# One written order for the whole first phase of an attention and expert kernel, with one v tile for the tail tokens of two batches

## The chip, the core and the metric

The kernel runs on one NeuronCore of one Trainium2 chip. The metric is device time in microseconds (us). The engines are PE (TensorE; its weight loads are PEld), DVE (VectorE), ACT (ScalarE), POOL (GpSimd) and SP, whose queue issues nearly all DMAs. Each engine takes its instructions in the order in which they stand in its queue.

## What is computed

Three layers follow each other, for 4 batches of 576 tokens:

```python
# 1. attention, 8 heads of 64, causal window of 128, ALiBi bias
scores = q @ k.T / 8 + slope * -(t - s)      # masked outside 0 <= t-s < 128
x = softmax(scores) @ v                      # [4, 576, 512]
# 2. gated layer
h = relu(x @ w_in); u, v = h[..., :512], h[..., 512:]
v_n = (v - mean(v)) / sqrt(var(v) + 1e-6)    # per token
v_s = w_spatial @ v_n + b_spatial            # mixes the 576 tokens
y = (u * v_s) @ w_out
# 3. four experts of full causal attention, gated by the top 2 logits
out = sum_e gate_e * (softmax(causal(q_e k_e.T / 8)) @ v_e) @ wo_e
```

All products run in a split of two parts (high and low) and three passes (high by high, high by low, low by high; `PASSES`, line 37), except the attention of layer 1 and the transposes.

## The kernel before

576 tokens are four tiles of 128 and a tail of 64 (`TOK`, line 34). A tile of layer 1 is (batch b, tile j), 20 of them. **The first phase** does layer 1 and the part of layer 2 up to the product u * v_s, which goes to DRAM (`g_dram`). **The fold** (`fold`, line 800 and after) multiplies w_out into the expert weights. **The second phase** does layer 3.

In the first phase each tile passes through these steps, with the names that the written order gives them: scores on PE (`s`, psum `ps`, two buffers), row minimum on DVE and exponential on ACT (`l`, `e`), division (`f`, three DVE instructions), transposes on PE (`t`, psum `pt`) and their copy on ACT (`c`), masking by POOL (`g`), the product with v (`a`, psum `px`), and the split of the result into x high (`xh`, ACT, line 498) and x low (`xl`, DVE, line 164). `pt` and `px` share a pool of one buffer (`psT`): transposes cannot start while an earlier `px` is still being read by `xh` and `xl`. Then layer 2: `V`, 12 products of 512 columns for each tile of 128 tokens (line 524), `r`, `bn`, `ag`, `n`, `N` (relu, mean and variance, normalising and splitting on ACT and DVE), `U` (288 columns, 12 products for each of four feature blocks and two halves of the tokens, line 588) and `P` (the mixing over tokens, 14 products each, lines 615 and 618), with `pm` multiplying by u. Opening work beside this: `C0` to `C7` decode the eight chunks of w_in from 64-bit numbers and split them (two ACT copies, five DVE steps and three products each), `W` splits w_spatial, and four chunks of w_out are decoded in the same way.

Two things set the order. `OPENING` is a text of single steps in the order of issue; all engines follow it, up to about tile 6. After it a loop over the remaining tiles (lines 730 and after) issues attention steps at fixed places, and between them pulls V, U and P products from a list (`Dense`, whose `pull` hands out work by estimated cost). There only PE follows the program's order; the queues of ACT, DVE, POOL and SP are ordered by a scheduler that simulates the program when it is built. `out_weights` (four chunks of w_out) is one of the things that the loop steps through. `idle` and `warm` add transposes of the identity, whose results are not used.

A tail tile has 64 tokens, but its V products are as long as those of a whole tile: the 64 tokens stand twice among the 128 columns of the loaded operand (`take`, the 640-column `x`), since the second copy is needed by the mixing in split form.

Of the kernel before, what the change touches and what calls it, by code (L numbers as in the profile page):

```python
# [37 lines left out]
OPENING = """
    k0 q0 q1 raw0 raw1 raw2 raw3 k1 k3 k4 k5 s0.0 s0.1 C0.abs v0 l0.0.0 l0.1.0 e0.0.0 C0.max e0.1.0 l0.0.1 C0.shl v1 C1.abs l0.0.2 C0.or e0.0.2 e0.0.1
    C1.max C0.sum+17 v2 C0.mask l0.0.3 C0.mul e0.0.3 l0.1.1 C2.abs C0.add raw4 f0.0.add l0.1.2 f0.0.rec l0.1.3 C0.high f0.0.mul s1.1+2 v3 e0.1.2 C1.shl  # L40
    e0.1.3 k2 C2.max C0.minus e0.1.1 t0.0 v4 l1.1.cp C0.low s1.0 f0.1.add C1.or c0.0 f0.1.rec l1.1.0 C1.sum f0.1.mul e1.1.0 l1.0.cp t0.1 l1.1.1 q2 c0.1
    l1.1.2 l1.1.3 l1.0.0 e1.1.1 q3 l1.0.1 a0 e1.0.0 l1.0.2 l1.0.3 e1.0.1 q4 C1.mask C2.shl e1.0.3 reltail C1.mul xh0 e1.0.2 C2.or C1.add e1.1.2 f1.0.add
    xl0 C2.sum C3.abs raw5 e1.1.3 f1.0.rec C2.mask C1.high f1.0.mul C3.max C1.minus t1.0 f1.1.add C2.mul C1.low c1.0 f1.1.rec C3.shl raw6 s2.1+2 C4.abs
    f1.1.mul C3.or s2.0 C4.max C3.mask t1.1 q5 C4.shl C3.sum l2.0.cp g1.0.0 c1.1 C4.or C2.add C2.high l2.1.cp g1.1.0 C4.sum g1.0.1 l2.0.0 l2.0.1 e2.0.0
    C2.minus l2.0.2 g1.1.1 l2.0.3 e2.0.1 l2.1.0 l2.1.1 C2.low C4.mask a1+4 e2.1.1 C3.mul e2.1.0 C4.mul raw7 C5.abs l2.1.2 W0.ld e2.0.2 l2.1.3 C5.max
    C3.add e2.1.2 W1.ld s4.0 e2.1.3 C5.shl v5 C3.high C5.or s4.1 C6.abs f2.1.add l4.0.cp C3.minus xh1 f2.1.rec C5.sum C5.mask f2.1.mul C3.low C4.add
    e2.0.3 C6.max V0.0 C4.high C5.mul f2.0.add C6.shl V0.1 C7.abs f2.0.rec xl1 W0.hi C5.add C7.max W1.hi C4.minus f2.0.mul t2.1 C5.high V0.2 W1.lo c2.1
    C7.shl C4.low C5.minus W0.lo t2.0 r0 V1.0 C7.or C5.low W2.ld c2.0 bn0 g2.1.0 W3.ld C7.sum g2.0.0 l4.0.0 ag0 l4.0.1 e4.0.0 V1.1 l4.1.cp g2.1.1 e4.0.1
    l4.1.0 l4.1.1 g2.0.1 e4.1.0 f4.0.add s3.1 f4.0.rec e4.1.1 C7.mask C6.or a2 C7.mul W2.hi C6.mask W3.hi l3.1.cp V1.2 W3.lo xh2 v6 C6.mul C7.add r1
    C6.sum l3.1.0 l3.1.1 C7.high l3.1.2 l3.1.3 s5.1 e3.1.1 f4.0.mul e3.1.3 C7.minus f4.1.add xl2 C6.add e3.1.0 s3.0 f4.1.rec e3.1.2 W2.lo C7.low t4.0  # L50
    f3.1.add f4.1.mul W4.ld C6.high V2.0 f3.1.rec l3.0.cp W5.ld c4.0 f3.1.mul q6 t4.1 C6.minus c4.1 V2.1 q7 l3.0.0 g4.0.0 C6.low l3.0.1 g4.1.0 l3.0.2
    e3.0.0 l3.0.3 g4.0.1 t3.1 l5.1.0 e3.0.1 l5.1.1 g4.1.1 U0.2.0 l5.1.2 e3.0.2 l5.1.3 bn1 e3.0.3 U0.2.1 c3.1 U0.0.0 f3.0.add ag1 f3.0.rec e5.1.0 f3.0.mul
    U0.2.2 e5.1.3 g3.1.0 s6.1 e5.1.2 e5.1.1 g3.1.1 W5.hi t3.0 f5.1.add l6.1.cp U0.0.1 f5.1.rec l6.1.0 U0.0.2 c3.0 f5.1.mul e6.1.0 s6.0 W5.lo ur0.0 ur0.2
    l6.1.1 g3.0.0 W4.hi V2.2 l6.1.2 l6.1.3 e6.1.2 l6.0.cp g3.0.1 a4 e6.1.3 W4.lo e6.1.1 r2 f6.1.add l6.0.0 s5.0 f6.1.rec xh4 l6.0.1 bn2 U0.1.0 e6.0.1 q8
    xl4 U0.1.1 e6.0.0 U0.1.2 f6.1.mul t5.1 ag2 l6.0.2 ur0.1 l6.0.3 U0.3.0 n2.ln l5.0.0 c5.1 l5.0.1 U0.3.1 l5.0.2 e6.0.3 l5.0.3 U0.3.2 e6.0.2 e5.0.1 a3
    f6.0.add e5.0.3 f6.0.rec f6.0.mul e5.0.2 ur0.3 n2.ex e5.0.0 n2.r0 V4.0 n2.r1 xh3 v7 f5.0.add n2.r2 f5.0.rec n2.r3 f5.0.mul v8 V4.1 xl3 N0.sc V4.2
    N1.sc N0.hi N2.sc t5.0 N1.hi N0.lo V3.0 c5.0
"""
# [1159 lines left out]
```

## Time and profile before

| | |
|---|---|
| median of 3 runs (lowest, highest) | 497.64 us (497.02, 500.23) |
| profiled execution, its own time | 497.51 us |
| its span, first to last instruction | 495.8 us |
| PE busy (share of the span) | 480.6 us (97%) |
| DVE, ACT, POOL busy | 305.5, 262.7, 101.2 us |
| mean granted TensorE clock | 0.993 |

The span is what the trace shows; the execution's own time is 1.7 us longer. "Busy" of PE counts a matmul until its modelled end, and matmuls overlap, so the distance from the start of one matmul to the start of the next tells what it costs. A number in brackets after "idle before" or behind an arrow says how long an engine stood idle and which instruction ended that.

### The profile page before, as it was taken

How to read it: one execution, taken by the hardware profiler on the slowest of the kernel's cores; microseconds unless marked ns; L12 is line 12 of the kernel's file. 1: busy time of each engine (PE TensorE's matmuls, PEld its weight loads, DVE VectorE, ACT ScalarE, POOL GpSimd, SP SyncE). 2: the span in 40 equal slices, each digit the busy share in tenths (PEclk: the TensorE clock that was granted, in tenths of full speed). 3: DMA queues.
4: the chain of work that ended last, by engine and by line, in shares of the span. 5: the costliest groups of instructions: out<-in, count | busy, mean ns of one | idle time of the engine just before them, and what ended most of it. 6: DMA issues, size and time to landing. Idle time of an engine off the chain costs nothing.

```text
span 495.8 us, 10569 instructions
## 1 busy us (share of the span) xinstructions
PE 480.6 (97%) x3919; PEld 422.5 (85%) x3919; DVE 305.5 (62%) x1082; ACT 262.7 (53%) x782; POOL 101.2 (20%) x210
## 2 busy tenths in 40 slices
PE   7889999999999998999999999999999999999997
PEld 6467789997889987899888999998899899897875
DVE  3899888645977657775455524365484564556352
ACT  3777976523655445653345314256575545545554
POOL 3032402211202221021211010112322243223110
PEclk9899999999999998999999999999999999999999
DMA  7963233145204431300305550330000000001223
GB/s 240 342 189 118 82 97 117 47 134 173 66 32 141 149 138 42 98 25 27 111 1 189 190 189 2 97 96 1 2 23 2 2 22 1 1 1 66 85 86 107
DMA packets 24631, 43.77 MB, mean 88 GB/s; under 512 B 5634, under 2 KB 8066, under 8 KB 24196
## 3 DMA queue, kind: packets, MB, share of 16 engines
q1 hardware_dynamic: 24436, 42.97, 26.4%
q8 instruction: 31, 0.51, 0.4%
q14 instruction: 20, 0.16, 0.1%
q10 hardware_dynamic: 144, 0.13, 0.1%
HBM read 31.55 MB, written 11.53 MB: 87 GB/s over the span
## 4 chain that ended last, share of the span: by engine, by line
PE 84%; DVE 7%; DMA 3%; ACT 3%; SPq 2%; issue 1%; ACTq 0%
PE pg L615 10%; PE pq L910 10%; PE pv L524 10%; PE pu L588 7%; PE pvB L934 6%; PE pxB L1042 5%; PE pout L1077 5%; PE ptB L1021 5%; PE px L486 5%; PE psB L975 4%; PE ps L411 4%; PE pw L809 3%; PE pt L455 3%; PE pg L618 2%; DMA q<-in_qP 2%; DMA k<-in_kP 2%
## 5 line engine op out<-in xcount | busy, mean ns | idle before, releaser
L187 ACT ACTIVATE p<-p,st 128x128 f32<-128x128 f32 x144 | 56.3, 393 | 26.5 <-DVE st L186 26.3
L524 PE MATMUL pv<-win,x 128*128 128x512 f32 x240 | 63.1, 404 | 0.7 <-ACT x L498 0.7
L910 PE MATMUL pq<-x,W 128*128 128x288 f32 x384 | 58.3, 302 | 0.8 <-DVE k L164 0.8
L615 PE MATMUL pg<-wsp,vn 128*128 128x288 f32 x384 | 58.9, 298 | 0.0
L588 PE MATMUL pu<-x,win 128*128 128x288 f32 x384 | 57.1, 304 | 0.0
L910 PEld LDWEIGHTS pq<-x,W 128*128 128x128 f32 x384 | 52.0, 189 | 3.6 <-DVE k L164 1.5
L464 POOL TENSOR_SCALAR_AFFINE_SELECT pU<-pT 128x512 f32<-128x512 f32 (+1 forms) x32 | 23.2, 726 | 154.5 <-ACT pT L457 144.2
L588 PEld LDWEIGHTS pu<-x,win 128*128 128x128 f32 x384 | 53.6, 193 | 1.2 <-ACT vn L557 0.3
L615 PEld LDWEIGHTS pg<-wsp,vn 128*128 128x128 f32 x384 | 52.9, 188 | 1.3 <-issue 1.3
L524 PEld LDWEIGHTS pv<-win,x 128*128 128x128 f32 x240 | 43.1, 188 | 11.4 <-issue 1.8
L199 POOL TENSOR_SCALAR pB<-pB,stB 128x384 f32<-128x384 f32 (+4 forms) x64 | 36.0, 582 | 70.3 <-DVE stB L998 53.8
L187 ACT ACTIVATE pB<-pB,stB 128x128 f32<-128x128 f32 (+3 forms) x64 | 35.6, 558 | 20.3 <-DVE stB L186 20.3
L934 PE MATMUL pvB<-W,x 128*128 128x260 f32 (+1 forms) x240 | 34.3, 289 | 0.0
L186 DVE CUSTOM_DVE_ANT_0 pB<-psB,trit 128x128 f32<-128x128 f32 (+3 forms) x64 | 28.2, 485 | 9.6 <-PE psB L975 9.2
L186 DVE CUSTOM_DVE_ANT_0 p<-ps,relm 128x128 f32<-128x128 f32 x128 | 29.9, 284 | 5.2 <-PE ps L411 4.6
L934 PEld LDWEIGHTS pvB<-W,x 128*128 128x128 f32 (+1 forms) x240 | 29.9, 178 | 1.7 <-issue 1.7
L411 PE MATMUL ps<-k,q 64*128 64x256 f32 (+1 forms) x256 | 30.6, 374 | 0.5 <-DMA q<-in_qP 0.5
L1021 PE MATMUL ptB<-ident,pB 128*128 128x128 f32 (+1 forms) x200 | 31.0, 275 | 0.0
L457 ACT COPY pT<-pt 128x512 f32<-128x512 f32 (+1 forms) x40 | 21.6, 540 | 15.5 <-PE pt L455 14.5
L1077 PE MATMUL pout<-wo,o 128*128 128x512 f32 x102 | 29.3, 412 | 0.0
L536 DVE BATCH_NORM_STATS2 vs<-vr 128x6 f32<-128x512 f32 x20 | 13.8, 692 | 24.0 <-ACT vr L533 24.0
L1042 PE MATMUL pxB<-pTB,vt 128*64 128x128 f32 (+2 forms) x480 | 28.3, 262 | 0.0
(162 smaller groups left out, 894.4 us busy)
## 6 DMA issues: line engine op xcount, KB each, us to landing
q<-in_qP SPq DMA_DIRECT2D x20, 256.0 KB, 2.9
g_dram<-g SPq DMA_DIRECT2D x16, 288.0 KB, 2.1
...
```

Of the source, the lines that this page charges most:

```text
L186: lambda: nc.vector.tensor_tensor_reduce(s_view, ps_view, tab, -0.125, FLT_MAX, ALU.add, ALU.min, nm),
L187: lambda: nc.scalar.activation(s_view, s_view, AF.Exp, bias=nm, scale=-1.0, accum_out=sm),
L199: nc.gpsimd.tensor_scalar(p, p, r, 0.0, op0=ALU.mult, op1=ALU.add)
L411: nc.tensor.matmul(ps[:, o, 256 * h : 256 * h + kn], Q_[b, j][r, hp, :], K_[b][r, hp, k0 : k0 + kn], start=True, stop=True)
L524: nc.tensor.matmul(pv, x[i][:, k, t0 : t0 + P], win[j][:, k, 512:1024], start=(n == 0 and k == 0), stop=(n == 2 and k == 3))
L588: nc.tensor.matmul(pu[:, :HALF], win[i][:, k, m * P : (m + 1) * P], x[j][:, k, c], start=(n == 0 and k == 0), stop=(n == 2 and k == 3))
L615: nc.tensor.matmul(pg[:, :HALF], vn[i][k][:, m * P : (m + 1) * P], wsp[j][:, k, c], start=(n == 0 and k == 0), stop=False)
L910: nc.tensor.matmul(pq[:, :HALF], W[i][:, k, c0 : c0 + P], G[j][:, k, c], start=(n == 0), stop=(n == 11))
L934: nc.tensor.matmul(pv[:tn, :260], G[i][:, k, COL[t] : COL[t] + tn], W[j][:, k, 512:772], start=(n == 0), stop=(n == 11))
L1021: nc.tensor.transpose(pt[:kb, n, :], p[pr][:, o, c0 : c0 + kb], ident)
L1042: nc.tensor.matmul(px[64 * o : 64 * o + 64, pr, :qn], vt[:kb, c, (2 * pr + o) * 64 : (2 * pr + o) * 64 + 64], rhs, start=(c == 0), stop=(c ...
L1077: nc.tensor.matmul(po[:tn], o2[i][:, pr, :tn], wos[j][:, pr, :], start=(n == 0), stop=(n == 5))
```

## The change

**The written order covers the whole first phase.** `OPENING` now has 1286 steps instead of 414 and ends at the last tile; `FIRST` and `SECOND` hold the rest (the last V, U and P products). The loop over tiles, `v_tile`, `u_half`, `spatial`, `normalised`, `out_weights` and `now`/`xready` are gone. Up to the end of `OPENING` every queue (ACT, DVE, POOL, SP) follows the text. Step names carry the batch now (`V0.4.2` is batch 0, tile 4, pass 2), `gs` is the store of u * v_s, and `O` are the steps of w_out's chunks. At the start the SP queue loads the first chunk of w_in ahead of the first two q tiles, and k of batch 1 behind w_in's seventh chunk instead of its fourth.

**Tail tokens of two batches share one V tile.** Odd batches run their tail first (`ORDER`). x has 704 columns: the tail stands at columns 0 to 63 (so that U reads 576 columns in a row) and again at 576 to 639 for an even batch, 640 to 703 for an odd one. V of tile 4 of batch 0 covers both tails, likewise batch 2; there is none for batches 1 and 3. The normalised rows go to four tiles `vt2` by ACT and DVE copies of halves. w_spatial and b_spatial are rolled by 64 on the way in, and u * v_s is read back by one DMA instead of two.

```diff
+ORDER = ((0, 1, 2, 3, 4), (4, 0, 1, 2, 3))
 OPENING = """
...
+    k0 raw0 q0 q1 raw1 raw2 raw3 k2 v0 T1 T0 C0.abs v1 C0.max C0.shl s0.1+10 v2 C0.or s0.0 l0.1.0 l0.1.1 C0.sum e0.1.0 l0.1.2 l0.0.0 e0.1.1 k1 l0.0.1
...
```

```diff
-    x = [xg.tile([P, 4, 640], F32R, name=f"x{i}") for i in range(2)]
+    x = [xg.tile([P, 4, 704], F32R, name=f"x{i}") for i in range(2)]
     u = [d2.tile([P, S], F32, name=f"u{m}") for m in range(4)]
-    vn = [[d2.tile([P, 512], F32R, name=f"vn{i}_{t}") for t in range(5)] for i in range(2)]
-    back, over = u[0][:, :P], u[1][:, :P]
+    vn = [[d2.tile([P, 512], F32R, name=f"vn{i}_{t}") for t in range(4)] for i in range(2)]
+    vt2 = [[d2.tile([P, 512], F32R, name=f"vt{r}_{i}") for i in range(2)] for r in range(2)]
+    back, over, first = (u[i][:, :P] for i in range(3))
+    nc.gpsimd.affine_select(out=first, in_=back, pattern=[[-1, P]], fill=FAR, **below)
+    for h in range(H):
+        nc.vector.tensor_scalar(relm[:, 0, h, :], first, -8.0 * 2.0 ** -(h + 1.0), None, op0=ALU.mult)
...
                 nc.sync.dma_start(K_[b][:, :, q0 : q0 + qn], kP[b, :, :, q0 : q0 + qn])
-            elif j == 0:
+            elif j == ORDER[b % 2][0]:
         if "v" in parts:
-            V_[b, j] = a1.tile([P, 512], F32, tag="v", name=f"v{b}_{j}", bufs=5)
-            if j == 4:
-                nc.gpsimd.memset(V_[b, j][qn:], 0.0)
-            nc.sync.dma_start(V_[b, j][:qn], v[b, q0 : q0 + qn])
+            for t in ((j,) if b % 2 == 0 or j < 3 else (3, 4) if j == 4 else ()):
+                t0, tn = TOK[t]
+                kept = b % 2 and t > 2
+                V_[b, t] = vtail[b % 2] if t == 4 else a1.tile([P, 512], F32, tag="w" if kept else "v", name=f"v{b}_{t}", bufs=1 if kept else 5)
+                nc.sync.dma_start(V_[b, t][:tn], v[b, t0 : t0 + tn])
...
     def take(b, j, px, parts=(0, 1)):
         q0, qn = TOK[j]
         if j < 4:
-            to = [t[:, :, q0 : q0 + P] for t in x]
+            to = [t[:, :, 64 + q0 : 64 + q0 + P] for t in x]
         else:
-            to = [t[:, :, 512:640].rearrange("p m (r c) -> p m r c", r=2) for t in x]
+            to = [t.rearrange("p m (r c) -> p m r c", c=64)[:, :, 0 : 10 + b % 2 : 9 + b % 2, :] for t in x]
             px = px[:, :, :64].unsqueeze(2).to_broadcast([P, 4, 2, 64])
         if 0 in parts:
             nc.scalar.copy(to[0], px)
         if 1 in parts:
             lo_part(to[1], px, to[0])
-            xready[b, j] = now[0]
...
-        t0 = TOK[t][0]
+        t0 = 64 + TOK[t][0]
...
         def high(t):
-            nc.scalar.copy(vn[0][t], vr[t])
+            if t < 4:
+                nc.scalar.copy(vn[0][t], vr[b, t])
+                return
+            both, odd = vt2[0][1], slice(64, 128)
+            nc.scalar.copy(both, vr[b, t])
+            nc.scalar.copy(vt2[0][0][0:64], vr[b, t][0:64])
+            for i in range(2):
+                nc.scalar.copy(vt2[1][i][0:64], vr[b, t][odd])
 
+            if t < 4:
+                lo_part(vn[1][t], vr[b, t], vn[0][t])
+                return
+            both, odd = vt2[0][1], slice(64, 128)
+            lo_part(vt2[1][1][odd], vr[b, t][odd], both[odd])
+            lo_part(both[odd], vr[b, t][0:64], both[0:64])
...
-                    nc.tensor.matmul(pg[:, :HALF], vn[i][4][:kn, m * P : (m + 1) * P], wsp[1 - i][:kn, 4, c], start=False, stop=(i == 1))
+                    nc.tensor.matmul(pg[:, :HALF], vt2[b % 2][i][:kn, m * P : (m + 1) * P], wsp[1 - i][:kn, 4, c], start=False, stop=(i == 1))
...
-    tiles = [(b, j) for b in range(B) for j in range(5)]
-    ops_ = {}
+    tiles = [(b, j) for b in range(B) for j in ORDER[b % 2]]
...
     with tc.manual_schedule(engines={E_.Activation, E_.DVE, E_.Pool, E_.SP}):
-        warm(28)
+        warm(15)
         for name in OPENING.split():
             step(name)
-    decoded[0] = 9
-    for name, names in (("u0_0", FIRST), ("u0_1", SECOND), ("s0", THIRD)):
+    for name, names in (("u3_1", FIRST), ("s3", SECOND)):
         dense.add(rest(names), cost(names), name=name)
-    for b in range(1, B):
...
-    def parts(s):
-
-        if s >= 9:
-            next(outw, None)
-
-    RATE = 8200.0
-    outw = iter(())
-    for s in range(7, len(tiles) + 2):
-        now[0] = 4 * s
-
-        tc.no_sync_barrier()
-        if s == 9:
-            early_stack.close()
-            outw = out_weights(right.enter_context(tc.tile_pool(name="later", bufs=1, side="right")))
-        if s > 2:
-            b, j = tiles[s - 2]
-            if j in (0, 2) and b > 0:
-                dense.through(f"u{b - 1}_{j // 2}")
-            px = attend(b, j)
-        if s < len(tiles):
-            scores(*tiles[s])
-        if s > 2:
-            take(*tiles[s - 2], px)
-        if 4 <= s + 2 < len(tiles):
-            load_chunk(*tiles[s + 2])
...
-        nc.sync.dma_start(f[:, :, 64:576], src[:, :, 0:512])
-        nc.sync.dma_start(f[:, :, 0:64], src[:, :, 512:576])
+        nc.sync.dma_start(f, src)
```

(The new `out_ops` issues the same instructions for a chunk of w_out as `out_weights` did, one step each.)

PE, the last V tiles of the program (`pv`; x high and low are x_106 and x_107, w_in's two parts win_102 and win_103). Before, batch 3 ends with its tail tile:

```order
L524 MATMUL pv_4_3181<-win_102,x_106 128x512 x4
L524 MATMUL pv_4_3181<-win_103,x_106 128x512 x4
L524 MATMUL pv_4_3181<-win_102,x_107 128x512 x4
L588 MATMUL pu_0_1_3200<-x_106,win_102 128x288 x4
L588 MATMUL pu_0_1_3200<-x_107,win_102 128x288 x4
L588 MATMUL pu_0_1_3200<-x_106,win_103 128x288 x4
```

Now the last V tile is tile 3 of batch 3, between two passes of a P product (`pg`):

```order
L555 MATMUL pv_3_3114<-win_102,x_106 128x512 x4
L555 MATMUL pv_3_3114<-win_103,x_106 128x512 x4
L555 MATMUL pv_3_3114<-win_102,x_107 128x512 x4
L633 MATMUL pg_3_0_3056<-wsp_104,vn_0_116 128x288
L633 MATMUL pg_3_0_3056<-wsp_104,vn_1_117 128x288
L633 MATMUL pg_3_0_3056<-wsp_104,vn_2_118 128x288
L633 MATMUL pg_3_0_3056<-wsp_104,vn_3_119 128x288
L636 MATMUL pg_3_0_3056<-wsp_105,vt_0_120 128x288
L636 MATMUL pg_3_0_3056<-wsp_104,vt_1_121 128x288
L618 MATMUL pu_0_1_3144<-x_106,win_102 128x288 x4
L618 MATMUL pu_0_1_3144<-x_107,win_102 128x288 x4
L618 MATMUL pu_0_1_3144<-x_106,win_103 128x288 x4
```

In all, PE has 240 products in V before and 216 now.

PE, from the product with v of tile (2, 3) on (`px_3`). Before, the next user of the same psum buffer is the transpose `pt_4`:

```order
L486 MATMUL px_3_2296<-pT_3_1_2241,v_3_1689 64x128 x2
L411 MATMUL ps_0_0_2313<-k_2017,q_0_2015 128x128 x4
L411 MATMUL ps_0_1_2318<-k_2017,q_0_2015 128x128 x4
L588 MATMUL pu_0_0_2290<-x_107,win_102 128x288 x4
L588 MATMUL pu_0_0_2290<-x_106,win_103 128x288 x4
L588 MATMUL pu_1_0_2344<-x_106,win_102 128x288 x4
L455 MATMUL pt_4_0_2349<-ident,p_4_0_2214 128x128 x2
L588 MATMUL pu_1_0_2344<-x_107,win_102 128x288 x4
```

Now:

```order
L529 MATMUL px_3_2311<-pT_3_1_2146,v_3_1505 64x128 x2
L555 MATMUL pv_2_2286<-win_102,x_107 128x512 x4
L462 MATMUL ps_0_1_2339<-k_1414,q_0_1873 128x128 x4
L462 MATMUL ps_1_1_2347<-k_1414,q_1_2046 128x256 x4
L529 MATMUL px_4_2355<-pU_4_0_2259,v_3_1505 64x64 x2
L529 MATMUL px_4_2355<-pT_4_0_2258,vtail_162 64x64 x2
```

The scores of the next tiles and a pass of V stand between `px_3` and the next user of the buffer, which is now another `px`, that of the tail tile.

DVE, where w_out's first chunk is decoded (`wo`, `fo`, `rawo`). Before, the first of these steps stand behind the products with u of batch 0 (`g`):

```order
L621 TENSOR_TENSOR g_1_1223<-u_109,pg_1_0_1224 128x288
L438 TENSOR_TENSOR p_3_1_1287<-p_3_1_1287,st_3_1_1288 128x512
L621 TENSOR_TENSOR g_1_1223<-u_109,pg_1_1_1255 128x288
L621 TENSOR_TENSOR g_2_1281<-u_110,pg_2_0_1282 128x288
L621 TENSOR_TENSOR g_2_1281<-u_110,pg_2_1_1313 128x288
L329 TENSOR_SCALAR fo_1432<-fo_1432 128x512
L330 TENSOR_SCALAR wo_1431<-fo_1432 128x512
L164 TENSOR_TENSOR x_107<-px_2_1340,x_106 128x4x128
```

Now the chunk's steps stand ahead of the division of the tail tile of batch 1 (`p_4_0`, `p_4_1`), among the normalising of batch 0 (`vs`, `vr`):

```order
L579 SCALAR_TENSOR_TENSOR vs_458<-vs_458 128x3
L384 SCALAR_TENSOR_TENSOR wo_719<-rawo_658,wo_719 128x512
L580 TENSOR_TENSOR vs_458<-vs_458 128x3
L385 TENSOR_SCALAR fo_720<-wo_719 128x512
L581 TENSOR_SCALAR vs_458<-vs_458 128x3
L487 TENSOR_TENSOR st_0_0_786<-st_0_0_786,tiny 128x4
L386 SCALAR_TENSOR_TENSOR fo_720<-rawo_658,fo_720 128x512
L582 TENSOR_TENSOR vs_458<-vs_458 128x3
L213 TENSOR_TENSOR x_107<-px_3_792,x_106 128x4x128
L586 TENSOR_SCALAR vr_1_586<-vr_1_586,vs_458 128x512
```

The chunk moved from among batch 0's P products to a place ahead of all of them.

## Rows read from the trace of the kernel before

**Rows 1.** The page: span, and busy time of each engine.

```profile
span 495.8 us, 10569 instructions
...
PE 480.6 (97%) x3919; PEld 422.5 (85%) x3919; DVE 305.5 (62%) x1082; ACT 262.7 (53%) x782; POOL 101.2 (20%) x210
```

**Rows 2.** Timeline of PE, opening: start, length, engine, line, operation, tiles, count.

```profile
39.75 0.39 PE L279 MATMUL psw<-win,minus 128*128 128x512 f32 x1
39.98 0.60 PE L455 MATMUL pt<-ident,p 128*128 128x128 f32 x4
40.33 1.17 PE L524 MATMUL pv<-win,x 128*128 128x512 f32 x4
...
45.09 1.13 PE L411 MATMUL ps<-k,q 64*128 64x256 f32 x8
46.15 0.44 PE L486 MATMUL px<-pU,v 128*64 128x128 f32 x4
...
48.05 1.19 PE L524 MATMUL pv<-win,x 128*128 128x512 f32 x4
...
70.20 3.02 PE L524 MATMUL pv<-win,x 128*128 128x512 f32 x12
73.05 0.60 PE L455 MATMUL pt<-ident,p 128*128 128x128 f32 x4
```

**Rows 3.** Groups of instructions: shape, count, busy us, mean ns, idle us before.

```profile
L524 PE MATMUL pv<-win,x 128*128 128x512 f32 x240 | 63.1, 404 | 0.7 <-ACT x L498 0.7
```

**Rows 4.** Waits of PE: total us, times, longest us.

```profile
PE pt L455 <- DVE x L164: 4.0, 4, 2.1
...
PE pv L524 <- ACT x L498: 0.7, 1, 0.7
```

**Rows 5.** Chain of waits, 180 to 200 us: start, length, what.

```profile
186.68 1.45 DVE vr L554 x3
188.13 0.60 DVE wo L331
188.73 0.60 DVE vn L164
...
189.76 0.61 DVE x L164
...
190.50 0.41 PE pt L455 x2
```

**Rows 6.** Two stretches: busy us by engine, TensorE clock, DMA share.

```profile
core 0: us, PE busy (x) PEld busy (x) DVE busy (x) ACT busy (x) POOL busy (x), PEclk, DMA share, GB/s
12.40:62.00 49.60, 46.40 (x294) 32.07 (x295) 45.49 (x170) 38.94 (x122) 12.38 (x16) 0.97 0.58 183
186.00:198.40 12.40, 10.32 (x68) 9.71 (x66) 9.84 (x35) 7.37 (x26) 2.10 (x4) 0.86 0.14 42
```

**Rows 7.** Timeline of DVE, opening.

```profile
30.54 0.69 DVE L429 COPY_PREDICATED ps<-lowt,ps 128x512 f32<-128x512 uint16 x1
31.13 0.28 DVE L186 CUSTOM_DVE_ANT_0 p<-ps,relm 128x128 f32<-128x128 f32 x1
31.34 0.28 DVE L186 CUSTOM_DVE_ANT_0 p<-ps,relm 128x128 f32<-128x128 f32 x1
...
38.13 0.15 DVE L436 TENSOR_TENSOR st<-st,tiny 128x4 f32<-128x4 f32 x1
38.20 0.42 DVE L330 TENSOR_SCALAR u<-f 128x512 int32<-128x512 int32 x1
38.54 0.16 DVE L437 RECIPROCAL st<-st 128x4 f32<-128x4 f32 x1
```

**Rows 8.** Timeline of ACT and DVE: the first chunk of w_in.

```profile
9.88 0.69 ACT L328 ACTIVATE f<-raw 128x512 f32<-128x512 f32 x1 [7.28 <-DMA raw<-in_w_in]
...
10.60 0.43 DVE L329 TENSOR_SCALAR f<-f 128x512 f32<-128x512 f32 x1 [1.57 <-ACT f L328]
```

**Rows 9.** Timeline of PE: the first product of the weight fold.

```profile
287.98 12.23 PE L809 MATMUL pw<-wc,wt 128*128 128x386 f32 x68
```

More of the change, by code (lines that the diff above doesn't have):

```diff
@@ L42 @@
[L42 to L53, printed above, removed]
@@ L237, in block_kernel @@
         nc.gpsimd.memset(pad[r : r + 1, :], 1.0)
+    for r in range(2):
+        nc.gpsimd.tensor_scalar(vt2[r][0][64:97], pad[64:97].to_broadcast([33, 512]), 1.0, 0.0, op0=ALU.mult, op1=ALU.add)
     early_stack = ExitStack()
-    decoded = [0]
     early = early_stack.enter_context(tc.tile_pool(name="early", bufs=4, side="right"))
@@ new lines, in out_ops, with get, start, high @@
+    def out_ops(k, pool):
+        c = slice(k * P, (k + 1) * P)
+        wide = w_outT.dtype == I64
+        wide = w_outT.dtype == I64
+        raw = pool.tile([P, 512], w_outT.dtype, tag="raw", name=f"rawo{k}", bufs=2)
+        ops, tiles = {}, {"w": raw}
+        def get(n, dtype, tag="f", bufs=3):
+            tiles[n] = pool.tile([P, 512], dtype, tag=tag, name=f"{n}o{k}", bufs=bufs)
+            return tiles[n]
+        def start():
+            if wide:
+                w, f = get("w", F32, "w", 2), get("f", F32)
+                ops.update(word_ops(w, f, raw, f))
+                ops["abs"]()
+        def high():
+            nc.scalar.copy(get("hi", F32R), tiles["w"])
+        def low():
+            lo_part(get("lo", F32R), tiles["w"], tiles["hi"])
+        for n in ("max", "shl", "or", "mask", "mul"):
+            ops[n] = lambda: None
+        ops["ld"] = lambda: nc.sync.dma_start(raw, w_outT[c, :])
+        ops["add"] = lambda: nc.vector.tensor_add(tiles["w"], tiles["w"], tiles["f"]) if wide else None
+        ops["sh"] = lambda: nc.sync.dma_start(wt_dram[0, k], tiles["hi"].bitcast(F32))
+        ops["sl"] = lambda: nc.sync.dma_start(wt_dram[1, k], tiles["lo"].bitcast(F32))
+        ops["abs"], ops["hi"], ops["lo"] = start, high, low
+        return ops
@@ L374, in block_kernel @@
     Q_, K_, V_ = {}, {}, {}
+    vtail = [a1.tile([P, 512], F32, name=f"vtail{i}", bufs=1) for i in range(2)]
+    for t in vtail:
+        nc.gpsimd.memset(t[64:], 0.0)
     def load_chunk(b, j, parts="qkv"):
@@ L439, in softmax_ops @@
         return ops
-    def softmax(b, j, g):
-        for op in softmax_ops(b, j, g).values():
-            op()
     def transpose_ops(b, j, g):
@@ L467, in transpose_ops @@
         return ops
-    def transposes(b, j, g):
-        for op in transpose_ops(b, j, g).values():
-            op()
     def attend(b, j):
@@ L569, in normal_ops @@
         return ops
-    def normalised(st, tiles):
-        ops = normal_ops(st, tiles)
-        yield lambda: (ops["ln"](), ops["ex"]())
-        yield lambda: [ops[f"r{i}"]() for i in range(4)]
-        for t in tiles:
-            for name in ("sc", "hi", "lo"):
-                yield ops[f"{name}{t}"]
     def u_ops(b, s, m):
```

256 lines of the change are left out of this document (117 added, 139 removed).

## The prediction

> **What bounds the kernel now.** I read the busy times first: PE is busy for 480.6 of 495.8 us, DVE for 305.5 [rows 1]. The reader is to see that all other engines have room on average, so a change pays what it takes off PE's queue, and costs what it makes PE wait. Second, the timeline of PE in the opening gives prices that the busy times don't: the distance from one start to the next, since matmuls overlap [rows 2]. Third, the waits of PE: transposes wait four times, 4.0 us in all and 2.1 at the longest, for DVE's x low, and V once, 0.7 us, for ACT's x high [rows 4]. Fourth, the chain of waits around the longest of them shows why: x low at 189.76 stands in DVE's queue behind the scaling of three V tiles, a step of w_out's decoding and a split of V; the transposes that want its buffer start at 190.50 [rows 5]. Fifth, the table of stretches: from 186.0 to 198.4 the granted clock averages 0.86, so after this wait PE was at 1.2 GHz for a share of 0.28 of it and did (1 - 0.86) x 12.4 = 1.7 us less work than at 2.4 [rows 6]. In the opening it is different: from 12.4 to 62.0 us DVE is busy for 45.49 of 49.6 us, 4.1 idle, and PE's early work hangs on it [rows 6].
>
> All sums are made against the profiled execution's own 497.51 us, 1.7 above its span and 0.1 below the median of 497.64.
>
> **Part 1: 24 products of V less.** The instruction lists have 240 and 216. Twelve such products take 73.05 - 70.20 = 2.85 us, 0.2375 each [rows 2]; busy time over count gives 63.1 / 240 = 0.263 [rows 3]. So 24 are worth 5.7 to 6.3 us; I take 5.7, since the distance between starts is what PE's queue pays. V lies on PE's queue in stretches that DVE and ACT don't hold up, so all of it counts. The relu, statistics and scaling that go with two dropped V tiles, and the extra half copies into vt2, are on ACT and DVE after the opening and hide behind PE, which is busy there without a break.
>
> The Trainium skill ("TensorE: Matmul & The Clock Gate", section "Back-to-back issue gap") gives some 131 ns for a 512-column product in a sustained stream. By that the part would be worth 24 x 0.131 = 3.1 us and the sum 490.2; this trace does not agree, with 237 ns.
>
> **Part 2: the waits of PE behind the loop.** At the place of the longest wait the old order leaves two score groups and three U passes between `px_3` and the transposes; the new one leaves a pass of V (0.95) and two score groups, one of them whole at 46.15 - 45.09 = 1.06 [rows 2], at least 2.4 us. What must fit in is x high and x low; x low takes 0.61 [rows 5], and x high I put at the same length, so 1.3 us with the handing over. The order in which ACT and DVE take them matters more than the room: old x low stood behind five other DVE instructions, because only PE was held to the program there. In the written text, for tiles 9 to 19, I added up PE's work between each `a` and the next use of the buffer: never under 1.9 us (after a9 and a12), and x low has at most a few instructions ahead of it. So the waits should go. Bounds: nothing goes (0), or all goes: 4.0 + 0.7 [rows 4] + 1.7 of clock [rows 6] = 6.4. I take 5.0, near the upper end, and leave 1.4 for new short waits, since twenty hand-overs on fixed queues will not all be met. With PE no longer stopped for 2.1 us the clock should hold; if some other stop of that length appears, the 1.7 comes back.
>
> **Part 3: the opening.** Here PE follows DVE, so I compare how far DVE's queue is ahead of PE's at the points where PE needs it. Distances on DVE: a 512-column step 31.13 - 30.54 = 0.59, the fast kind 38.54 - 38.20 = 0.34, a row minimum 0.21, a small one 0.07, say 0.08 [rows 7]. On PE: a score group 1.06, the product with v 48.05 - 46.15 = 1.9, a conversion pass 0.23, a turn 0.35, a V pass 0.95 [rows 2]. Before, the largest lead is at the transposes of the tail tile (t4.1): ahead of them DVE has 39 long, 24 fast, 32 minima and 18 small ones, 23.0 + 8.2 + 6.7 + 1.4 = 39.3 us; PE has 11 score groups (five of them short, 0.5), 25 filling transposes (0.09), 31 conversion passes (0.24), seven turns, three products with v (tile 0's is 1.0) and seven V passes, 32.3 us. Lead 7.0. Now it is at the tail tile of batch 1 (t5.1), which V of the shared tile needs: DVE has 59 long, 27 fast, 44 minima and 33 small ones, 55.8 us, w_out's first chunk among them; PE has 15 score groups (eight short), 27 fillers, 32 conversion passes, eleven turns, five products with v, twelve V passes and six U passes (0.53, by columns), 47.2 us. Lead 8.6, so PE waits 1.6 us longer. Against it: the first chunk of w_in lands at 9.88 now and DVE stood idle 1.57 us for it [rows 8]; two q loads no longer stand ahead of it on SP's queue, which gives back between nothing and 1.6. I take the middle, +0.8. Bounds: DVE's 4.1 idle us [rows 6] and the 1.6 with them may shrink or double, -4 to +6. The shorter warm-up (28 to 15) and other fillers stand where PE waits for the first data; I cost them at nothing, covered by that wait.
>
> **Costed at nothing.** K of batch 1 behind more of w_in, and the stores `gs` on SP's queue, ahead of loads of tiles that are wanted at least a tile later. The pads on POOL (101.2 us busy) [rows 1]. The rolled weights (on the way in) and one DMA instead of two for reading back, which end under the last P products.
>
> **Sum.** 497.5 - 5.7 - 5.0 + 0.8 = 487.6 us.
>
> **The rivals.**
> (a) The waits come back elsewhere: part 2 gives 0, with part 3 at +0.8 to +2.4. Time 492.6 to 494.2. For it: ACT and DVE queues that are fixed can hold PE at other tiles; against it: the room counted above. Chance 0.20.
> (b) The opening gets shorter too: DVE's sum up to the last decoding step of the half of w_in that V reads falls from 20.9 (18 long, 15 fast, 22 minima, 8 small) to 15.5 us (13, 12, 16, 4), so V can begin some 5 us earlier. If a good half of that survives the later lead, part 3 is -3; with part 2 at its full 6.4: 497.5 - 5.7 - 6.4 - 3.0 = 482.4. For it: the idle 4.1 us of DVE; against it: the lead of 8.6, which no earlier V removes. Chance 0.14.
> (c) Slower: one late step on a fixed queue holds all behind it. The place is the hand-over px, x high, x low, next use of the buffer, in all 20 tiles; the price is what the four recorded waits cost on average, 1.0 us [rows 4]. If all 20 paid it, 20 - 4 = 16 us more and the clock loss stays: 497.5 - 5.7 + 0.8 + 16 = 508.6. It decides from the fifth waiting tile more than now: 497.5 - 5.7 + 0.8 leaves 4.9 us to lose. For it: a tile waits now with 2.6 us of PE work between (two short score groups and three U passes); against it: DVE is free for 38% of the span [rows 1]. Chance 0.10.
> (d) The dropped products are worth half their distance, because those that stay then stand as far apart as their neighbours' weight loads demand: 24 x 0.119 = 2.9 us, 490.4 in sum. Against it: the twelve in the row stand 237 ns apart. Chance 0.04.
> (e) That the change doesn't do what it says: the instruction lists show 24 products fewer and the new order on every queue, so only an unnoticed reordering of the parts after the opening text remains; it has no price of its own and no chance here.
> The forecast, 484.5 to 491.5, has 0.52.
>
> **The numbers.** 487.6 us; range 482.5 to 495.0, which takes in the forecast, (a), (d) and about half of (b), some 0.83. About 1%, 5 us, is what a measurement of this kernel can tell: faster below 492.7, from the forecast, (b), (d) and a part of (a): 0.73; within 1%, most of (a) and the mild end of (c): 0.19; slower 0.08.
>
> **What would show it.** Part 1: 216 products in V's group and still 230 to 240 ns from start to start. Part 2: the wait of transposes for x low gone from PE's list, and no second stretch at 1.2 GHz after the opening. Part 3: the first product of the shared V tile is reached with PE's total wait in the opening within 2 us of the old one. Together: the fold's first product, at 287.98 before [rows 9], starts near 278; what follows it is unchanged in code, so nearly the whole difference must stand there. The prediction is wrong if PE shows new waits of over 3 us in sum behind the opening, if the fold starts later than 283, or if the second phase changes by more than 1 us.

## The result and the profile after

| | before | after |
|---|---|---|
| median (lowest, highest) | 497.85 us (497.02, 500.23), 4 runs | 483.7 us (483.63, 485.17), 4 runs |
| profiled execution, its own time | 497.51 us | 483.76 us |
| its span | 495.8 us | 482.0 us |
| PE busy | 480.6 us | 471.5 us |

The ratio is 0.9715, 95% interval 0.9677 to 0.9753. The change takes 13.8 us off the profiled execution, against 9.9 forecast: 483.7 is in the range and 3.9 below the 487.6.

The page of the changed kernel, for [rows 1]: PE's share is 98% now, DVE's work is nearly the same, and in the 40 slices of the granted clock none is below 9.

```profile
span 482.0 us, 10496 instructions
...
PE 471.5 (98%) x3884; PEld 413.5 (86%) x3884; DVE 304.2 (63%) x1084; ACT 262.3 (54%) x780; POOL 95.0 (20%) x206
...
PEclk9999999999999999999999999999999999999999
```

The fold's first product, for [rows 9] (duration minimum, median, maximum, then the first and the last start):

```profile
L773 PE MATMUL pw<-wc,wt x96: 333/339/344, 274.2 to 291.0; 128*128 128x386 f32 x96
```

It starts at 274.2 in place of 287.98, so all of the 13.8 us stand ahead of it. What follows is as long as before: 482.0 - 274.2 = 207.8 us against 495.8 - 287.98 = 207.8.

The longest waits of PE, for [rows 4]:

```profile
PE psw L328 <- DVE st L487: 1.7, 1, 1.7
PE warm L347 <- POOL ident masks.py:199: 1.6, 1, 1.6
PE ps L462 <- DMA q<-in_qP: 0.9, 1, 0.9
PE pq L873 <- DVE k L213: 0.8, 1, 0.8
PE pt L502 <- ACT pT L504: 0.5, 1, 0.5
```

Neither the transposes' wait for x low nor V's for x high is there. Of these rows only `pq` lies behind 62 us, in the second phase: from 62.0 to the fold the list of PE's waits is empty, and the table of stretches shows PE busy for the whole of it (columns as in [rows 6]; the first row answers to the opening there, the second to the place of the old longest wait):

```profile
12.40:62.00 49.60, 47.38 (x353) 33.65 (x353) 47.33 (x172) 39.23 (x122) 10.39 (x16) 1.00 0.74 256
186.00:198.40 12.40, 12.40 (x119) 11.17 (x118) 8.38 (x39) 7.91 (x32) 1.67 (x4) 1.00 0.01 2
...
62.00:274.20 212.20, 212.20 (x1731) 191.86 (x1730) 141.08 (x483) 110.88 (x348) 32.77 (x58) 1.00 0.27 92
```

The group of V, for [rows 3], and a run of 12 of its products on PE's timeline, for [rows 2]:

```profile
L555 PE MATMUL pv<-win,x 128*128 128x512 f32 x216 | 56.1, 400 | 0.0
```

```profile
37.08 3.02 PE L555 MATMUL pv<-win,x 128*128 128x512 f32 x12
39.94 0.60 PE L502 MATMUL pt<-ident,p 128*128 128x128 f32 x4
```

24 products fewer, and (39.94 - 37.08) / 12 = 0.238 us each, as before.

DVE's first work, for [rows 7, 8]. Before, a first part of it stands in [rows 8]: the first step of w_in's chunk at 10.60 us, after 1.57 us without work. Ahead of that there was a longer gap, which the prediction has no row for:

```profile
2.64 1.21 DVE L227 TENSOR_SCALAR relm<-u 128x128 bf16<-128x128 f32 x8
8.40 0.29 DVE L186 CUSTOM_DVE_ANT_0 p<-ps,relm 128x128 f32<-128x128 f32 x1 [4.55 <-PE ps L411]
```

After:

```profile
4.60 2.00 DVE L280 TENSOR_SCALAR relm<-u 128x128 bf16<-128x128 f32 x8
6.82 0.43 DVE L382 TENSOR_SCALAR f<-f 128x512 f32<-128x512 f32 x1 [0.22 <-ACT f L381]
```

DVE begins on the chunk at 6.82 us, 3.8 earlier, and stands idle for 0.22 us there instead of 4.55 + 1.57 = 6.1. V's first product, before and after:

```profile
37.55 2.12 PE L524 MATMUL pv<-win,x 128*128 128x512 f32 x8
```

```profile
28.58 3.02 PE L555 MATMUL pv<-win,x 128*128 128x512 f32 x12
```

It starts 9.0 us earlier. PE's idle time in the first 62 us is the same, 6.5 us: PE is busy for 55.45 of them before and for 55.48 after.

### The profile page after: what moved, and what is told of

The parts are those of the page before. It is cut to its first block, busy times and chain, and to the rows that moved or that the text cites. A ratio compares the mean times of both kernels' runs of the same rounds, so it can differ in the third digit from the quotient of the medians.

```text
span 482.0 us, 10496 instructions
## 1 busy us (share of the span) xinstructions
PE 471.5 (98%) x3884; PEld 413.5 (86%) x3884; DVE 304.2 (63%) x1084; ACT 262.3 (54%) x780; POOL 95.0 (20%) x206
## 4 chain that ended last, share of the span: by engine, by line
PE 91%; issue 3%; DVE 2%; POOL 1%; DMA 1%; ACT 1%; SPq 0%; POOLq 0%; ACTq 0%
PE pu L618 11%; PE pg L633 11%; PE pq L873 10%; PE pv L555 9%; PE pvB L897 6%; PE px L529 6%; PE pxB L1005 6%; PE pout L1040 5%; PE ps L462 5%; PE ptB L984 5%; PE psB L938 4%; PE pw L773 4%; PE pt L502 3%; PE pg L636 2%; PE psB L940 1%
## 5 line engine op out<-in xcount | busy, mean ns | idle before, releaser
L511 POOL TENSOR_SCALAR_AFFINE_SELECT pU<-pT 128x512 f32<-128x512 f32 (+1 forms) x32 | 20.8, 653 | 182.9 <-ACT pT L504 182.8
L555 PE MATMUL pv<-win,x 128*128 128x512 f32 x216 | 56.1, 400 | 0.0
L555 PEld LDWEIGHTS pv<-win,x 128*128 128x128 f32 x216 | 38.7, 188 | 8.2 <-issue 1.3
L641 DVE TENSOR_TENSOR g<-u,pg 128x288 f32<-128x288 f32 x32 | 14.4, 451 | 23.6 <-PE pg L636 23.6
L462 PEld LDWEIGHTS ps<-k,q 64*128 64x128 f32 x256 | 20.9, 186 | 8.7 <-issue 5.6
```

What stands on the lines that cost most here:

```text
L462: nc.tensor.matmul(ps[:, o, 256 * h : 256 * h + kn], Q_[b, j][r, hp, :], K_[b][r, hp, k0 : k0 + kn], start=True, stop=True)
L555: nc.tensor.matmul(pv, x[i][:, k, t0 : t0 + P], win[j][:, k, 512:1024], start=(n == 0 and k == 0), stop=(n == 2 and k == 3))
```

## The experiments

Twelve kernels ran, in three groups on three chips. The kernel before had medians of 496.5, 496.7 and 496.6 us there, and the changed kernel, run once more in the second group, 484.2 (483.57 to 484.37), ratio 0.9744 (0.9721 to 0.9767), fold again at 274.2. The start of the fold in the profiled execution stands beside each median; it holds that one execution's stretches at 1.2 GHz, too.

> The changed kernel once more, unedited, as the reference for the other runs here: 482.5 to 484.5, ratio to the kernel before 0.968 to 0.975, no wait of transposes for x low and the fold's first product near 274.

### The dropped products: v_back and before_v_less

```diff
-... V1.3.2 ... V3.3.2 ...
+... V1.3.2 V1.4.0 V1.4.1 V1.4.2 ... V3.3.2 V3.4.0 V3.4.1 V3.4.2 ...
```

> The changed kernel with 24 products of V put back (12 behind V of tile 3 in batches 1 and 3, their results unread). Theory: each costs its distance, 0.2375 us, so 5.7 us more: 489.4. Rival (d) of the prediction: half the distance, 2.9 us: 486.6. Second rival: they fall into time in which PE would wait anyway, under 1 us: 483.7 to 484.7.

490.37 us (490.08 to 490.81), ratio 0.9884 (0.9864 to 0.9904); the fold starts at 280.9, 6.7 us later. Between 62 us and the fold PE has one wait, which the changed kernel has not:

```profile
PE pv L555 <- ACT vr L564: 0.7, 1, 0.7
```

At that place the products stand 0.85 us further apart than usual, and 0.27 us of the delay stand ahead of the first product put back (V of tile 3 starts its last pass at 137.27 in place of 137.00). 6.7 - 0.85 - 0.27 = 5.6, or 0.23 us for each of 24. Rival (d) and the third theory fall.

The same products taken out of the kernel before:

```diff
             for k in range(4):
-                nc.tensor.matmul(pv, x[i][:, k, t0 : t0 + P], ...)
+                if t < 4 or b % 2 == 0:
+                    nc.tensor.matmul(pv, x[i][:, k, t0 : t0 + P], ...)
+                elif n == k == 0:
+                    nc.tensor.matmul(pv, ..., start=True, stop=True)
```

> The kernel before with 22 of the 24 V products of the tail tiles of batches 1 and 3 left out (one stays of each tile, and the rest of the computation is as it was, on wrong statistics of those rows). Theory: the distance of each, 0.2375 us, comes off: 5.2 us, 492.3 to 492.6, with the waits for x low still there (4.0 us) and a second stretch at 1.2 GHz. Rival: as PE's work between the product with v and the next user of its buffer shrinks, waits grow into the room, and only 2 to 3.5 us come off: 494 to 496. Rival (d): half the distance, 2.6 us, 495.0, with waits unchanged.

496.9 us against 496.5, ratio 1.0013 (0.9996 to 1.0031): nothing comes off, less than even the rival had. Its waits of PE between 62 us and the fold:

```profile
PE pt L455 <- DVE x L164: 5.8, 4, 2.4
PE pv L527 <- ACT x L498: 0.7, 1, 0.7
PE pt L455 <- ACT pT L457: 0.7, 1, 0.7
PE pu L591 <- ACT vr L536: 0.4, 1, 0.4
PE pg L621 <- POOL vn L568: 0.4, 1, 0.4
```

These are 8.0 us against 4.7 in [rows 4], 3.3 more, and a stretch of 3.4 us at 1.2 GHz follows the longest, one more than before behind the opening, for 1.7: together 5.0 us, against the 5.2 that PE no longer works. (The profiled fold starts at 286.6, 1.3 us earlier, but this execution was 1.7 ahead at 119.3 us, before the first product is left out: its opening ran at full clock. From there on it lost 0.4, so 0.6 of the loss stays unexplained.) DVE's timeline of this kernel shows what PE runs into, at the first hand-over behind the shortened tile:

```profile
141.70 1.00 DVE L557 TENSOR_SCALAR vr<-vr,vs 128x512 f32<-128x512 f32 x2
142.93 0.69 DVE L164 TENSOR_TENSOR vn<-vr,vn 128x512 fp32r<-128x512 f32 x1 [0.23 <-ACT vn L560]
143.54 0.42 DVE L332 TENSOR_SCALAR fo<-wo 128x512 int32<-128x512 int32 x1
144.00 0.69 DVE L164 TENSOR_TENSOR vn<-vr,vn 64x512 fp32r<-64x512 f32 x1
144.72 0.69 DVE L333 SCALAR_TENSOR_TENSOR fo<-rawo,fo 128x512 f32<-128x512 uint32 x1
145.44 0.98 DVE L360 TENSOR_TENSOR wo<-wo,fo 128x512 f32<-128x512 f32 x1
146.35 0.68 DVE L164 TENSOR_TENSOR x<-px,x 128x512 fp32r<-128x512 f32 x1
```

The product with v is issued at 139.87 there; x low comes at 146.35, behind a bunch of normalising and decoding steps without a gap. PE arrives earlier, DVE does not.

### The waits behind the opening: before_room, before_in_order, xl12_six

```diff
         now[0] += 1
-        dense.pull(RATE / 6)
+        dense.pull(RATE / 3)
         parts(s)
...
             parts(s)
-        dense.pull(RATE / 6)
```

> The kernel before with one edit in the loop: the list of dense work is pulled twice as far ahead of the first transposes of a tile (2733 in place of 1367 of its cost units), and not at the tile's end. So PE has about 1.3 us more work between the product with v and the next user of its buffer, while ACT, DVE and POOL are still ordered by the scheduler. Theory: the room was what was missing: the waits of transposes for x low fall from 4.0 us to under 1, the second stretch at 1.2 GHz goes, and 4 to 5.5 us come off: ratio 0.989 to 0.992. Rival: the room is not enough, since the order in which DVE takes x low is what holds it up, or work pulled early is missing later: under 1.5 us come off, ratio 0.997 or more.

498.16 us against 496.7, ratio 1.0034 (1.0016 to 1.0051), fold at 287.3. The waits for x low fall to 1.3 us and the second stretch at 1.2 GHz is gone, as the theory has it, but others have come, between 62 us and the fold:

```profile
PE pg L615 <- ACT u L591: 2.4, 1, 2.4
PE px L486 <- ACT pT L457: 1.7, 2, 0.9
PE pt L455 <- DVE x L164: 1.3, 2, 1.0
PE pv L524 <- ACT x L498: 0.7, 1, 0.7
```

The rival is right in its second form: one wait is filled, and the work is missing elsewhere.

```diff
-    for s in range(7, len(tiles) + 2):
+    with tc.manual_schedule(engines={E_.Activation, E_.DVE, E_.Pool, E_.SP}):
+        for s in range(7, len(tiles) + 2):
```

> The kernel before with the loop's ACT, DVE, POOL and SP queues held to the order of the program, too. The instruction lists show the same order on PE, DVE and POOL as without that, and some moved rows on ACT and SP alone. Theory now: x low came late on DVE because the loop's list hands out DVE's work in bunches ahead of it, not because a scheduler reordered it; so the waits for x low stay at 3.5 to 4.5 us and the time within 0.5% of the kernel before. Rival (as the prediction had it): holding the queues to the program takes the waits away, 4 us or more off, ratio 0.992 or less.

518.88 us (516.68 to 520.93), ratio 1.0445 (1.0418 to 1.0473), fold at 309.6: neither theory. The sentence on the instruction lists in the expectation is wrong, too: DVE's list differs from batch 0's splits of V on, with x low one place ahead of two of them and statistics ahead of row minima. PE's waits between 62 us and the fold:

```profile
PE pt L455 <- DVE x L164: 6.1, 4, 3.7
PE pg L618 <- POOL vn L565: 5.2, 2, 4.0
PE pu L588 <- ACT u L591: 2.0, 1, 2.0
...
```

Between 62 us and the fold PE is idle for some 19 us in all (4.7 before), and the granted clock averages 0.96 there (0.99 before). So the scheduler of the old loop was no loss: without it the loop's text is 22 us slower. Written text on fixed queues is not better by itself; this text is.

```diff
-            take(*tiles[num[0]], ops_["x", num[0]], ("hl".index(kind[1]),))
+            for _ in range(6 if name == "xl12" else 1):
+                take(*tiles[num[0]], ops_["x", num[0]], ("hl".index(kind[1]),))
```

> The changed kernel with x low of tile 12 written six times over in place of once (the same values), so that one hand-over of the shared psum buffer comes 5 x 0.61 = 3.1 us late. Between the product with v and the transposes that want the buffer PE has 14 products of P, 1.9 us, and x high and one x low need 1.3. Theory: PE waits there for 2.0 to 2.7 us, the clock falls to 1.2 GHz behind it as it did in the kernel before, and the whole costs 3.5 to 4.5 us: 487.2 to 488.2. Rival: the clock has nothing to do with the stop: 2.0 to 2.7 us, 485.7 to 486.4. Second rival: PE's later queue gives the wait back: under 1 us.

488.83 us (487.52 to 490.03) against 484.2, 4.6 more. PE's timeline and the granted clock behind it (the first number after the busy times' brackets), profiled execution of 490.03 us:

```profile
172.75 0.42 PE L636 MATMUL pg<-wsp,vt 97*128 97x288 f32 x2
176.27 0.66 PE L502 MATMUL pt<-ident,p 128*128 128x128 f32 x2 [3.09 <-DVE x L213]
```

```profile
175.60:182.40 6.80, 6.13 (x23) 4.92 (x24) 3.38 (x18) 2.70 (x13) 1.67 (x4) 0.50 0.15 40
```

The wait is 3.1 us, 0.4 above the upper bound, and the fold starts at 280.4, 6.2 us late: 3.3 for the stop and 2.9 for 6.8 us at 1.2 GHz. The five executions show the clock's share apart: 487.52 at a mean granted clock of 1.000, 488.8 to 488.9 at 0.996, 490.03 at 0.993. Against 483.6 to 483.8 at 1.000 the stop costs some 3.8 us, and the clock 0, 1.3 or 2.5 more. Of the 3.8, 0.5 is more than the profiled stop and has no explanation here. The theory holds as to the mechanism, with a cost just above its 4.5; the clock doesn't fall every time.

### The opening: raw0_third, before_raw0_first, early_dve, tuned

```diff
-    k0 raw0 q0 q1 raw1 raw2 raw3 k2 ...
+    k0 q0 q1 raw0 raw1 raw2 raw3 k2 ...
```

> The changed kernel with one edit: the SP queue loads both q tiles ahead of the first chunk of w_in again. Theory: the opening got shorter (about 2 us in PE's idle time) because DVE can begin on this chunk at 6.8 us instead of 10.6; with the chunk third, DVE is held up by it for 3.2 to 3.8 us, since the decoding stands ahead of the first row minima in its queue, and the kernel takes 2 to 3.8 us more than 483.7: 485.7 to 487.5, with the fold's first product at 276 to 278 instead of 274.2. Rival: the shorter opening comes from the order of the decoding (fewer DVE steps ahead of V's half of w_in) and not from when the chunk lands; then the kernel stays within 0.7 us of 483.7.

488.78 us (487.57 to 489.47), ratio 0.9849 (0.9827 to 0.987), fold at 278.8, 4.6 us late. DVE and PE in this kernel:

```profile
11.01 0.43 DVE L382 TENSOR_SCALAR f<-f 128x512 f32<-128x512 f32 x1 [4.41 <-ACT f L381]
```

```profile
PE psw L326 <- DVE u L384: 5.2, 1, 5.2
```

DVE starts 4.2 us later than at 6.82, and PE waits for the chunk's steps: its first product for the chunk starts at 12.68 in place of 8.49, also 4.2 later. A stretch at 1.2 GHz, 6.8 us long, follows, in which PE is busy for 5.35 us (granted clock 0.52); over it the delay grows by 0.4 only, to 4.6 (the two score groups behind it start at 27.56 in place of 22.97). The theory holds; the cost of 4.6 is 0.8 us above its upper bound. The other side, the kernel before with this order of loads:

```diff
-    k0 q0 q1 raw0 raw1 raw2 raw3 k1 ...
+    k0 raw0 q0 q1 raw1 raw2 raw3 k1 ...
```

> The kernel before with one edit: the first chunk of w_in is loaded ahead of the two q tiles, as in the change. Its DVE queue still takes two row minima ahead of the chunk's first step, and they wait for the scores. Theory (the gain needs both: the chunk first on SP's queue and its first steps ahead of the minima on DVE's): DVE's wait for the chunk, 1.57 us, goes, the wait for the first scores, 4.55 us, stays or grows by up to 0.7, and 0.4 to 1.5 us come off in the fold's start: 286.5 to 287.6 against 287.98. Rival: the place on SP's queue is all of it, 3.5 to 5 us off, 283 to 284.5.

494.83 us (493.62 to 495.4) against 496.6, ratio 0.9955 (0.9939 to 0.9971); the fold starts at 284.1, 3.9 us earlier. Not all of that is the edit's: the profiled execution of the kernel before ran a part of its opening at 1.2 GHz (first row; the granted clock is the third number from the end), and again behind the longest wait [rows 6], and this one did neither.

```profile
12.00:20.00 8.00, 7.12 (x28) 3.98 (x29) 6.65 (x25) 5.17 (x18) 0.00 (x0) 0.79 1.05 374
```

Between executions of equal granted clock, 493.6 and 493.8 at 0.999 and 1.000 stand against 494.5 to 495.5, and 494.7 to 495.4 at 0.996 against 495.2 to 496.5: some 1 us less, as the theory has it. DVE's wait for the scores stays and that for the chunk goes:

```profile
8.52 0.29 DVE L186 CUSTOM_DVE_ANT_0 p<-ps,relm 128x128 f32<-128x128 f32 x1 [4.67 <-PE ps L411]
...
9.06 0.42 DVE L329 TENSOR_SCALAR f<-f 128x512 f32<-128x512 f32 x1
```

Two attempts to go further. The first:

```diff
-    k0 raw0 q0 q1 raw1 ...
+    raw0 k0 q0 q1 raw1 ...
...
-        nc.vector.tensor_scalar(relm[:, 1, h, :], back, ..., None, op0=ALU.mult)
+        nc.gpsimd.tensor_scalar(relm[:, 1, h, :], back, ..., 0.0, op0=ALU.mult, op1=ALU.add)
```

> The changed kernel with an even earlier start of DVE: the first chunk of w_in is loaded ahead of k as well, and the eight tables for the later tiles are built by POOL in place of DVE. Theory (the opening follows the start of DVE on the first chunk): it begins at about 6.0 us in place of 6.8, and 0.3 to 1.0 us come off: 482.7 to 483.4. Rival: k comes later, the first scores with it, and nothing is gained: 483.5 to 484.5.

484.45 us (484.09 to 484.63) against 484.2, fold at 275.1. DVE starts the chunk at 5.78, but its second step, which writes the buffer that POOL's tables are read from, waits for them:

```profile
7.64 0.43 DVE L383 TENSOR_SCALAR u<-f 128x512 int32<-128x512 int32 x1 [1.43 <-POOL relm L280]
```

The rival's time, with another cause: the wait was moved to POOL.

The second:

```diff
-... a2 ... xh2 s4.1 ... a4 ... V0.3.0 ...
+... s4.1 a2 ... xh2 ... V0.3.0 a4 ...
```

> The changed kernel with two steps moved to fill PE's waits for POOL's masks: the second half of tile 4's scores ahead of the product with v of tile 2, and the product with v of tile 4 behind the first pass of V of tile 3. The trace has 0.9 and 0.36 us of waiting at these two places. Theory: PE's waits in the opening that are left are single hand-overs, each worth its length: 0.8 to 1.2 us come off, the fold starts at 273.0 to 273.4, time 483.0 to 483.4 against 484.2. Rival: V of tile 2 or the copy into x waits in their place, and nothing comes off.

484.13 us (483.91 to 484.6) and a fold at 274.5: nothing comes off. Both waits for POOL are gone. PE is 0.2 us ahead of the changed kernel at 48.7 us and level with it at 49.5, where a score group now waits for a row minimum. PE's short waits in the opening are not worth their length one by one: DVE is the next bound there.

### Moved steps on fixed queues: o0_late and o0_spread

```diff
-... O0.abs ... O0.max ... O0.shl ... O0.or ... O0.mask ... O0.mul ... O0.add ... f5.1.mul O0.hi l6.1.0 ... t5.1 ... c5.1 ...
+... f5.1.mul O0.abs O0.max O0.shl O0.or O0.mask O0.mul O0.add O0.hi l6.1.0 ... t5.1 ... c5.1 ...
```

> The changed kernel with the decoding steps of w_out's first chunk (six on DVE, two on ACT) moved from ahead of the division of the tail tile of batch 1 to behind it. The prediction's rule for the opening (PE follows DVE's lead, 8.6 us at that tile's transposes) says that PE waits 1.6 us there and gives it back: 482.1. Theory now: DVE began 4 us earlier and its lead costs PE nothing at that place, so the time stays within 0.5 us of 483.7.

490.01 us (489.59 to 490.33), ratio 0.9876 (0.9856 to 0.9896), fold at 280.4: 6.2 us later, and neither theory. `O0.hi`, an ACT copy that waits for the last of the six DVE steps, stands ahead of `c5.1`, the copy that frees the transposes' buffer, in both texts; now those DVE steps stood just in front of it, and it held up ACT:

```profile
70.91 0.62 ACT L343 CAST hio<-wo 128x512 fp32r<-128x512 f32 x1 [3.69 <-DVE wo L351]
```

PE waited 3.7 us at the next transposes, and a stretch at 1.2 GHz followed. The second try kept ACT clear of that:

```diff
-... O0.max ... O0.shl ... O0.or ... O0.mask ... O0.mul ... O0.add ... f5.1.mul O0.hi l6.1.0 ... O0.sh ... l6.1.3 ... l7.1.3 ... O0.lo ... O0.sl ... f6.1.mul ... xh5 ... xl5 ...
+... f5.1.mul l6.1.0 ... l6.1.3 O0.max O0.shl ... l7.1.3 O0.or O0.mask ... f6.1.mul O0.mul O0.add ... xh5 O0.hi O0.sh ... xl5 O0.lo O0.sl ...
```

> The changed kernel with the DVE steps of w_out's first chunk spread behind the division of the tail tile of batch 1, each pair behind a row minimum or division of tiles 6 and 7, and the ACT copy of its high part behind x high of tile 5, so that no copy of transposes stands behind it. It does what the earlier run with one block meant to do: DVE's queue ahead of that tile's transposes is 2.9 us shorter. Theory: DVE's lead costs PE nothing there now, so the fold starts within 0.5 us of 274.2 and the time is 483.7 to 484.7. Rival (the rule of the prediction): PE waits 1.6 us for that lead, and they come back: 272.6 and 482.6.

493.41 us (492.52 to 493.97), ratio 0.9929 (0.9914 to 0.9943), fold at 284.4: 10.2 us later. It shows in three views. SP's own waits (the queue's; total, times, longest), then ACT's and DVE's timelines:

```profile
SPq L350 <- DVE fo L321: 14.4, 1, 14.4
```

```profile
80.39 0.67 ACT L303 CAST wsp<-st_bias 32x576 fp32r<-32x576 f32 x1 [8.13 <-DMA st_bias<-in_bsp]
```

```profile
81.78 0.76 DVE L148 TENSOR_TENSOR wsp<-st_bias,bias_hi 1x576 fp32r<-1x576 f32 x1 [6.52 <-ACT bias_hi L304]
82.77 0.69 DVE L148 TENSOR_TENSOR x<-px,x 128x512 fp32r<-128x512 f32 x1 [0.24 <-ACT x L476]
```

The chunk's moved steps held its load buffer longer. The load of the third chunk of w_out (`O2.ld`) wants that buffer and stands early on SP's queue, so SP waited 14.4 us with the load of b_spatial behind it; ACT waited for b_spatial, x high of tile 5 stood behind that on ACT, x low behind it on DVE, and PE's transposes waited 7.7 us for x low. The two runs were to tell whether DVE's lead at the transposes of batch 1's tail costs PE anything. Their times don't, but the three traces do. In the changed kernel these transposes start at 65.09 and 66.37 us with no wait; with DVE's steps taken from in front of them they start at 65.81 and 67.08 (o0_late), 65.89 and 67.17 (o0_spread), without a wait either and no earlier. The lead cost PE nothing there.

## Why the prediction was right, and where its sizes were off

**Part 1 (5.7) was right in size, and its reason holds for the new order alone.** Put back, the products cost 0.23 us each. Taken out of the old order they gave nothing: "V lies on PE's queue in stretches that DVE and ACT don't hold up" is wrong for the loop, where PE ran into DVE's backlog. Parts 1 and 2 are no separate terms: in these two runs the saving of the first is had only where the second took the waits away.

The Trainium skill ("TensorE: Matmul & The Clock Gate", section "Back-to-back issue gap") has some 131 ns for a product of 512 columns; by that, an estimate, v_back would have cost 3.1 us. The trace and the run, with 238 and 232 ns, don't agree.

**Part 2 (5.0) was the full 6.4.** 4.0 and 0.7 us of waits are gone, no wait took their place up to the fold, and the clock's 1.7 came back: 1.4 us more than taken, the reserve for new waits that didn't come. The clock term is a matter of the single execution: executions of the kernel before with a granted clock of 1.000 took 494.5 to 495.5 us in the later groups, about half of the others, at 0.993, 496.1 to 497.5; the changed kernel at 1.000 takes 483.6 to 483.8. Full clock is more frequent with the change, not certain: six of its nine executions are at 0.999 or above, and four of 45 of the kernel before in those groups. Between executions at full clock the change is worth 10.7 to 11.9 us. And the reason given, that only PE was held to the program, fell: held to it on all queues, the loop was 22 us slower. x low came late because the loop hands out normalising and decoding in bunches ahead of it ([rows 5] and the rows of before_v_less), and the new text puts at most a few steps there.

**Part 3 (+0.8) had the wrong sign, and a term was missing beside it.** In the profiled executions the opening is 13.8 - 5.7 - 6.4 = 1.7 us shorter. The prediction's own [rows 6] has a granted clock of 0.97 in the opening of the kernel before, (1 - 0.97) x 49.6 = 1.5 us of work; no term takes it up, and the changed kernel has 1.00 there. How much of the 1.7 belongs to that one execution is told by variants whose text is the same up to V's first product, at 37.55 in the kernel before. before_v_less, then before_room:

```profile
35.95 2.11 PE L525 MATMUL pv<-win,x 128*128 128x512 f32 x8
```

```profile
36.47 2.12 PE L524 MATMUL pv<-win,x 128*128 128x512 f32 x8
```

before_in_order has 36.51. So 1.0 to 1.6 of the 1.7 is the opening of the profiled execution of the kernel before, and 0.1 to 0.7 is left for the change. Between executions at full clock part 3 is what 10.7 to 11.9 leave behind 5.7 and 4.7 (the waits of before_raw0_first at 0.999 are 4.7 as well): 0.3 to 1.5 us shorter.

Two steps failed. "Lead 8.6, so PE waits 1.6 us longer": at the place of that lead PE doesn't wait. And "two q loads no longer stand ahead of it on SP's queue, which gives back between nothing and 1.6": that bound came from the 1.57 us that DVE waited for the chunk [rows 8]. The 4.55 us in which DVE waited for the first scores were open as well, and eight more tables and the chunk's first steps, ahead of the row minima now, fill them: DVE starts on the chunk 3.8 us earlier. It takes both: in the old order the new place on SP's queue gave about 1 us, and taking it out of the new order cost 4.6. That the first scores came earlier is not it: in before_v_less they start at 6.16 us in place of 7.52, but DVE then waits 2.82 us for the chunk and begins on it at 10.50, 0.1 earlier only. With a lead that is 1.6 us longer and a start that is 3.8 earlier PE should wait up to 2.2 us less, against the 0.1 to 1.5 measured. The 3.9 by which the forecast was too high are 1.4 of part 2, 1.0 to 1.6 of the opening of that one execution, and 0.9 to 1.5 of part 3 itself.

**The rivals.** (b) came in part: part 2 is at its full 6.4 and V begins 9 us earlier, where it had 5. But of its 3.0 us in the opening only 1.7 came, most of them the slow opening of one execution, so that its sum of 482.4 lies near 483.7 is in part luck. (a) did not come; (d) is excluded by v_back. (c) did not come in this text, but its mechanism is real and its price was set too low: 1.0 us for each late hand-over, where two ways of moving one chunk's steps cost 6.2 and 10.2 and the whole loop on fixed queues 22.

**What was to show it** did: 216 products at 238 ns, no wait for x low, no slow stretch, PE's idle time in the opening the same (6.5 us), nothing changed behind the fold's start. That start, 274.2, is 3.8 earlier than the 278 named.
